# Masks and evictions moved, x transposed into token order, and router logits made by token

## The chip, the cores and the metric

The kernel runs on one core of a Trainium2 chip. The metric is the device time of one execution in microseconds (us); three runs were made and their median counts. Engines are named as in the profile: PE is TensorE, PEld its weight loads, DVE VectorE, ACT ScalarE, POOL GpSimd, SP the engine that issues most transfers.

## The reference

Attention with 4 batches, 8 heads, 576 positions and 64 columns per head; the first four heads see a window of 32 positions, the others every fourth position of a window of 128. Its output, 2304 tokens of 512 columns, goes through a mixture of 8 experts with one expert per token, and then through a pair of dense layers with a softplus between them.

```
mask_plain = (rel >= 0) & (rel < 32)
mask_dil = (rel >= 0) & (rel < 128) & (rel % 4 == 0)
x = softmax(where(mask, scale * q @ k.T, -1e9)) @ v     # (2304, 512)
logits = x @ w_gate;  e = argmax(logits)                # 8 experts
gate_w = softmax(logits)[e];  eom = sigmoid(x @ w_output_gate)
y = gate_w * eom[e] * (relu(x @ w1[e]) @ w2[e])
g = softplus(y @ w_in);  out = g @ w_out
```

## The kernel before

The attention is cut into 20 tiles: 4 batches b, five stretches w of 128 positions (the last has 64). A loop of 22 iterations runs them in a pipeline. Iteration i makes, in the order of the code: `scores` and `softmax` of tile i (products `s` on PE, maximum and subtraction on DVE), the transposes of the probabilities of tile i-1 (`pp`, evicted by ACT as `pt`), some units of the next batch's q and k (`pqk`), `exps` of tile i on ACT, `transpose_x` and `evict_x` of tile i-2 (`px` on PE, `xT` on ACT), then sums, values (`o` on PE) and `normalise` (`x` on DVE) of tile i-1, and the stores of x. A q/k unit transposes pieces of q or k on PE; `evict_qk` copies them to SBUF, k on ACT, q on DVE in batch 0 and in the dilated half, otherwise on ACT. The unit with y == 2 holds the last pieces of both q and k, and is evicted in four copies.

A tile of x has its rows in token order for heads 0 to 3, and in dilated order (row 32 r + m holds token 4 m + r) for heads 4 to 7. `px` is made of four products of 128 columns, c = 0 to 3; c = 2 and 3 belong to the dilated half.

The router handles the tiles in six groups, `GROUPS`: tiles 0 to 3, 4 to 7, 8 to 10, 11 to 13, 14 to 16 and 17 to 19, called groups 0 to 5 here and in the code. `logits_of` forms the logits `pl` with the 32 columns of `wg` standing still and the tile's x moving, in up to four column groups of PE side by side; c = 0, 1 and c = 2, 3 go to different columns of PSUM, since their tokens are in different orders. `logits` copies the first to `lt`, adds the second in token order, and has PE transpose the sum (`plt`). The generator `route` then makes, in small steps that the loop pumps between its own work, arg max, gate and rank of each token (`rmx`, `req`, `roh`, `rsel`, `prk`, `rgs`, `cumb`), and `rposi`. With rposi, POOL scatters one column per tile to `idx_dram` by an indirect DMA (L605). `W_LT` and `W_RANK` say how many steps a group's generator lets pass at two points.

After group 3's scatters POOL loads `idx` and gathers the first expert's rows (`xg`, L817). In the tail, group 5 is routed beside the products `xacc` that put rows of late tiles in place (L940, L992; `l` and `h` are the split operands of these); PE then goes on with the experts (`ph`, `py`) and from 395 us with the dense layers.

Of the kernel before, what the change touches and what calls it, by code (L numbers as in the profile page):

```python
# [11 lines left out]
F32 = mybir.dt.float32  # L12
# [4 lines left out]
ALU = mybir.AluOpType  # L17
# [4 lines left out]
P = 128  # L22
# [20 lines left out]
def attn_moe_softplus_kernel(ctx: ExitStack, tc: tile.TileContext, q, k, v, w_gate, w_ogate, w1, w2, w_in, w_out, out, dbg=None):  # L43
# [8 lines left out]
    NW = 5  # L52
# [63 lines left out]
            nc.sync.dma_start(wg[:, :, j * NE : (j + 1) * NE], w.rearrange("(c p) e -> p c e", p=P))  # L116

    def masks():
        nc.vector.tensor_copy(mask_0, mask_w)
        nc.vector.tensor_copy(mask_0[:32, 0], mask_w[:32, 1])  # L120

    def consts2():
        nc.gpsimd.memset(upper, 1.0)
# [172 lines left out]
    def transpose_qk(b, half, ti, y):  # L296

        own = b == 0 and (half, ti, y) in ((0, 0, 2), (1, 0, 2))  # L300
        ps = (ps_x0 if own else ps_t).tile([P, 512], F32, tag="x0" if own else "tp", name=f"pqk{b}{half}{ti}{y}")

        def to(t, y):
            dst = qT[b % 2][64 * y : 64 * y + 64, half] if t == 0 else kT[b % 2][64 * y : 64 * y + 64, half, :, y]
            return dst[:, :, :S].rearrange("q x (p j) -> q x p j", j=9)

        if y < 2:
            r = raw[b, half, ti].rearrange("p y e -> p (y e)")
            for j in range(4):
                c = 2 * D * (5 * y + j)  # L310
                nc.tensor.transpose(ps[:, P * j : P * j + P], r[:, c : c + 2 * D], identf)
            for o in range(2):
                src = ps[64 * o : 64 * o + 64].rearrange("q (j x p) -> q x p j", j=4, x=2)
                evict_qk(b, half, ti, to(ti, y)[:, :, :, y + o : y + o + 7 : 2], src)
        else:

            for t in range(2):
                r = raw[b, half, t].rearrange("p y e -> p (y e)")
                nc.tensor.transpose(ps[:, P * t : P * t + P], r[:, 8 * D : 10 * D], identf)
            for y in range(2):  # L320
                for t in range(2):
                    src = ps[64 * y : 64 * y + 64, P * t : P * t + P].rearrange("q (x p) -> q x p", x=2)
                    evict_qk(b, half, t, to(t, y)[:, :, :, 8 - 8 * y], src)

# [129 lines left out]
    def transpose_x(b, w):  # L454
        d = tl[b, w]
        x2 = d["x"].rearrange("q a h d -> q (a h d)")
        ps = ps_x0.tile([P, 512], F32, tag="x0", name=f"px{b}{w}")
        for c in range(4):
            nc.tensor.transpose(ps[:, P * c : P * c + P], x2[:, P * c : P * c + P], identf)
        d["xp"] = ps  # L460

    xT = {}
# [8 lines left out]

    def logits_of(*tiles_):

        for c in range(NC):
            for i in tiles_:
                g = next(g for g, (t0, t1) in enumerate(GROUPS) if t0 <= i < t1)
                j = i - GROUPS[g][0]
                if ("pl", g) not in xT:
                    xT["pl", g] = ps_t.tile([P, 2, P], F32, tag="tp", name=f"pl{g}")
                nc.tensor.matmul(  # L480
                    xT["pl", g][32 * j : 32 * j + 32, c // 2],
                    wg[:, c],
                    xT[g][:, j, P * c : P * c + P],
                    start=(c % 2 == 0),
                    stop=(c % 2 == 1),
                    skip_group_check=True,
                )

    def logits(g):
        n_ = GROUPS[g][1] - GROUPS[g][0]  # L490
        if g < G_FAST:
            logits_of(*range(*GROUPS[g]))
        pl = xT.pop(("pl", g))
        lt = xt_p.tile([P, P], F32, tag="lt", name=f"lt{g}")

        nc.vector.tensor_copy(lt[: 32 * n_], pl[: 32 * n_, 0])
        yield 0
        lt_ = lt[: 32 * n_].rearrange("q (m r) -> q m r", r=4)
        nc.vector.tensor_tensor(lt_, lt_, pl[: 32 * n_, 1].rearrange("q (r m) -> q m r", r=4), ALU.add)
        yield W_LT[g]  # L500
        pt = ps_t.tile([P, P], F32, tag="tp", name=f"plt{g}")
        nc.tensor.transpose(pt[:, : 32 * n_], lt[: 32 * n_], identf[: 32 * n_, : 32 * n_])
        xT[g] = pt.rearrange("q (j e) -> q j e", j=4)[:, :, : 2 * NE]
# [2 lines left out]

    K = {"rt": rt_p, "ixe": const}

    G_FAST, W_LT, W_RANK = 5, (6, 8, 1, 1, 1, 1), (8, 8, 3, 2, 2, 2)
    places, routed = {}, [0]  # L510

    scat = []
# [623 lines left out]
    for i in range(n + 2):  # L1136
        nqk = 0
        PUMP[0], PUMP[1] = (2, 1) if i < 12 else (4, 2) if i < n else (2, 2)
        if i == n - 5:
            rawx.close()  # L1140
            K["wr"] = rctx.enter_context(tc.tile_pool(name="wr", bufs=RB, side="right"))
        if i == n - 4:
            per0x.close()
            K["w1"] = rctx.enter_context(tc.tile_pool(name="w1", bufs=4, side="right"))
            pctx = ExitStack()
            for nm, bufs in (("xge", 4), ("sp0", 4), ("xl0", 5), ("sel", 4), ("rt2", 2)):
                K[nm] = pctx.enter_context(tc.tile_pool(name=nm, bufs=bufs, side="right"))
            K["slots"] = K["sel"].tile([P, CAPS[0]], F32, name="slots", bufs=1)
            nc.gpsimd.iota(K["slots"], [[1, CAPS[0]]], base=0, channel_multiplier=0, allow_small_or_imprecise_dtypes=True)
        if i < n:  # L1150
            b, w = tiles[i]
            if b + 1 < B:
                nqk = (QK_AT if b else QK_0)[w]
                if w == 0:
                    if b == 0:
                        fills(1)
                    todo += [(b + 1, *u_) for u_ in QK_UNITS]
            scores(b, w)
            softmax(b, w)
        if 1 <= i < n + 1:  # L1160
            transpose_p(*tiles[i - 1])
            evict_p(*tiles[i - 1])
        if i < n:
            pump()
        events(i, 0)
        some_qk(nqk - 1)
        if i < n:
            exps(*tiles[i])
        if 2 <= i:
            transpose_x(*tiles[i - 2])  # L1170
            evict_x(i - 2)
            pump()
        events(i, 1)
        if 1 <= i < n + 1:
            sums(*tiles[i - 1])
        events(i, 2)
        some_qk(min(nqk, 1))
        if 1 <= i < n + 1:
            values(*tiles[i - 1])
            normalise(*tiles[i - 1])  # L1180
        if i == 2:
            small_loads()
        if i < n and b + 1 < B:

            for half, heads in (((0, (0, 1)),), ((0, (2, 3)),), ((1, (0, 1)),), ((1, (2, 3)),), ())[w]:
                load_v(b + 1, half, heads)
            if w in (1, 3) and b + 2 < B:
                load_qk(b + 2, w // 2)
        events(i, 3)
        pump()  # L1190
        events(i, 4)
        pump()
        if i == n - 4:
            nc.vector.tensor_scalar(K["slots"], K["slots"], e0nt, None, ALU.add)
            K["rt"] = K["rt2"]
# [303 lines left out]
```

## Time and profile before

| what | value |
| --- | --- |
| time, median of 3 runs | 805.63 us (804.82 to 807.19) |
| the profiled execution | 805.44 us, span 803.7 us |
| PE busy | 767.2 us, 95% of the span |
| PEld busy | 690.7 us, 86% |
| DVE busy | 545.3 us, 68% |
| ACT busy | 478.8 us, 60% |
| POOL busy | 98.4 us, 12% |

The profile comes from one execution. Its instructions carry the line of the kernel and the names of the tiles; "idle before" is the time that an engine waited ahead of an instruction, and the arrow names what ended the wait. The chain of waits is followed back from the last instruction, at each step to what released it. Busy time is a union of overlapping instructions: PE's passes overlap, so the mean of one is longer than its share of the busy time. An F32 product can show as more than one pass in the records. A row of a stretch holds its bounds, its length, then busy time (instructions) of PE, PEld, DVE, ACT and POOL, the granted clock as a share of full, the DMA share and GB/s; asked for one line, only the engines that it uses.

### The profile page before, as it was taken

To read this page: it belongs to the slowest core of one execution; us is meant where nothing else is said; L and a number is where in the kernel's file an instruction comes from. 1 tells how busy PE (TensorE), PEld (TensorE's weight loads), DVE (VectorE), ACT (ScalarE), POOL (GpSimd) and SP (SyncE) were. 2 spreads that over 40 slices of the span, in tenths; PEclk is the share of its full clock that TensorE was granted. 3 is DMA by queue.
4 is the path that set the end of the run, shared out by engine and by line. 5 is a ranking of instruction groups with operands and counts; after the bars stand their busy time and mean duration, and the time that the engine had idled before them with its cause. 6 is when DMAs were issued, how large, how long until landed. Compare 5 with 4: busy or idle time off the path is not lost.

```text
span 803.7 us, 15090 instructions
## 1 busy us (share of the span) xinstructions
PE 767.2 (95%) x5542; PEld 690.7 (86%) x5543; DVE 545.3 (68%) x1098; ACT 478.8 (60%) x935; POOL 98.4 (12%) x124
## 2 busy tenths in 40 slices
PE   6998887899999999999999999999999999999996
PEld 5666655798999999999988999999999998999994
DVE  5766866773567877885688887766656656656552
ACT  4774623354656756666798877666546555555552
POOL 9502033321011011000000000020001001001001
PEclk7999999899999999999999999999999999999999
DMA  8979755366688999978624311310001001001001
GB/s 222 252 199 225 146 135 168 79 184 205 235 266 274 325 298 308 322 243 276 210 79 130 107 46 40 93 65 11 10 1 40 0 1 40 2 1 39 1 1 39
DMA packets 89039, 106.85 MB, mean 133 GB/s; under 512 B 29900, under 2 KB 64332, under 8 KB 88944
## 3 DMA queue, kind: packets, MB, share of 16 engines
q1 hardware_dynamic: 80448, 90.04, 37.7%
q0 software_dynamic: 3888, 10.12, 3.8%
q10 hardware_dynamic: 4608, 5.38, 1.9%
q8 instruction: 65, 1.06, 0.6%
q14 instruction: 30, 0.25, 0.1%
HBM read 85.03 MB, written 20.63 MB: 131 GB/s over the span
## 4 chain that ended last, share of the span: by engine, by line
PE 76%; issue 9%; ACT 5%; DVE 4%; DMA 4%; another core or an unknown queue 0%; POOL 0%; SPq 0%; ACTq 0%; POOLq 0%
PE pg L874 7%; PE pg L875 7%; PE pg L876 7%; PE q L1408 7%; PE q L1407 7%; PE q L1409 7%; PE s L364 3%; PE py L870 3%; PE py L871 3%; PE py L872 3%; PE ph L870 3%; PE ph L872 3%; PE ph L871 3%; PE o L419 2%; PE ph L874 1%
## 5 line engine op out<-in xcount | busy, mean ns | idle before, releaser
L874 PE MATMUL pg<-xhm,wh 128*128 128x384 f32 x384 | 129.5, 337 | 0.4 <-ACT l L1374 0.4
L875 PE MATMUL pg<-xlm,wh 128*128 128x384 f32 x384 | 129.6, 338 | 0.0
L876 PE MATMUL pg<-xhm,wl 128*128 128x384 f32 x384 | 129.4, 337 | 0.0
L707 DVE TENSOR_TENSOR wl<-wr,wh 128x1024 fp32r<-128x1024 f32 (+1 forms) x86 | 98.2, 1143 | 30.6 <-ACT wh L762 29.9
L1372 ACT ACTIVATE u<-pg 128x384 f32<-128x384 f32 x96 | 47.1, 491 | 116.7 <-PE pg L876 116.5
L1408 PE MATMUL q<-wl,gh 128*128 128x512 f32 x288 | 113.2, 393 | 0.0
L1407 PE MATMUL q<-wh,gh 128*128 128x512 f32 x288 | 113.0, 393 | 0.0
L1409 PE MATMUL q<-wh,gl 128*128 128x512 f32 x288 | 112.6, 391 | 0.0
L762 ACT CAST wh<-wr 128x1024 fp32r<-128x1024 f32 x74 | 77.2, 1049 | 15.0 <-DMA wr<-in_moe_w_dram 5.0
L1378 DVE TENSOR_SCALAR w<-u 128x384 f32<-128x384 f32 x68 | 24.6, 362 | 85.1 <-ACT u L1373 84.6
L874 PEld LDWEIGHTS pg<-xhm,wh 128*128 128x128 f32 x384 | 72.1, 188 | 4.9 <-ACT l L1374 1.0
L875 PEld LDWEIGHTS pg<-xlm,wh 128*128 128x128 f32 x384 | 72.0, 188 | 3.7
L876 PEld LDWEIGHTS pg<-xhm,wl 128*128 128x128 f32 x384 | 72.1, 188 | 0.0
L1416 POOL DMA_INDIRECT out_dram<-o,perm_sb x18 | 18.1, 1004 | 435.7 <-DVE o L255 303.0
L1380 DVE SCALAR_TENSOR_TENSOR u<-w,u 128x384 f32<-128x384 f32 x96 | 53.7, 559 | 21.6 <-ACT w L1376 19.3
L1409 PEld LDWEIGHTS q<-wh,gl 128*128 128x128 f32 x288 | 54.1, 188 | 12.3
L1407 PEld LDWEIGHTS q<-wh,gh 128*128 128x128 f32 x288 | 54.1, 188 | 8.6
L1408 PEld LDWEIGHTS q<-wl,gh 128*128 128x128 f32 x288 | 54.0, 188 | 8.2
L870 PE MATMUL ph<-xh,wh 128*128 128x392 f32 (+5 forms) x192 | 58.6, 305 | 1.6 <-ACT y L897 0.9
L1382 DVE TENSOR_TENSOR l<-l,u 128x384 f32<-128x384 f32 x96 | 53.5, 557 | 7.4
L870 PE MATMUL py<-hh,wh 128*128 128x312 f32 (+8 forms) x192 | 58.4, 304 | 0.0
L871 PE MATMUL py<-hl,wh 128*128 128x312 f32 (+4 forms) x192 | 57.3, 299 | 0.0
(204 smaller groups left out, 1722.9 us busy)
## 6 DMA issues: line engine op xcount, KB each, us to landing
wr<-in_moe_w_dram SPq DMA_DIRECT2D x64, 512.0 KB
praw<-in_moe_w_out_dram SPq DMA_DIRECT2D x12, 512.0 KB
raw<-in_q_dram SPq DMA_DIRECT2D x8, 576.0 KB
raw<-in_k_dram SPq DMA_DIRECT2D x8, 576.0 KB
x_dram<-x SPq DMA_DIRECT2D x36, 128.0 KB
x2r<-yT_dram SPq DMA_DIRECT2D x12, 384.0 KB
vP<-in_v_dram SPq DMA_DIRECT2D x16, 272.0 KB
praw<-in_moe_w_in_dram SPq DMA_DIRECT2D x8, 512.0 KB
```

The costliest lines, as they stand in the source:

```text
L707: e.tensor_tensor(lo, src, hi.bitcast(F32), ALU.subtract)
L762: (eng or nc.scalar.copy)(d[1], d[0])
L870: nc.tensor.matmul(ps if wide else ps[:, :cut], wh, xh if wide else xh[:, :cut], start=wide, stop=False, skip_group_check=True)
L871: nc.tensor.matmul(ps[:, :cut], wh, xl[:, :cut], start=False, stop=False, skip_group_check=True)
L874: nc.tensor.matmul(ps, wh, xh, start=(first and i == 0), stop=False)
L875: nc.tensor.matmul(ps, wh, xl, start=False, stop=False)
L876: nc.tensor.matmul(ps, wl, xh, start=False, stop=(last and i == k - 1))
L1380: nc.vector.scalar_tensor_tensor(u, w_, 1.0, u, ALU.subtract, ALU.subtract)
L1382: nc.vector.tensor_tensor(l, l, u, ALU.subtract)
L1407: nc.tensor.matmul(acc[b, t], gh[:, ts_], wh, start=(f == 0), stop=False)
L1408: nc.tensor.matmul(acc[b, t], gh[:, ts_], wl, start=False, stop=False)
L1409: nc.tensor.matmul(acc[b, t], gl[:, ts_], wh, start=False, stop=(f == NF - 1))
```

## The change

1. The two copies that make `mask_0` go from DVE to ACT.
2. The four evictions of a y == 2 unit are ordered q, q, k, k instead of q, k, q, k.
3. The products c = 2 and 3 of `px` are ordinary products against `turn`, the identity read in another column order, so that xT comes out in token order in all four parts.
4. `logits_of` sums all four c in one place of PSUM. The add in `logits` goes. For groups 3 to 5 (`G_ROWS` = 3) the tile's x stands still and 16 columns of `wg` move, so that the logits come out by token; for these groups the copy `lt` and the transpose `plt` go too.
5. `W_LT` and `W_RANK` of groups 1 and 2 change, and one unit of q/k in tile 4 comes earlier (`early`).

```diff
--- before.py
+++ after.py
@@ -116,8 +116,8 @@
             nc.sync.dma_start(wg[:, :, j * NE : (j + 1) * NE], w.rearrange("(c p) e -> p c e", p=P))
 
     def masks():
-        nc.vector.tensor_copy(mask_0, mask_w)
-        nc.vector.tensor_copy(mask_0[:32, 0], mask_w[:32, 1])
+        nc.scalar.copy(mask_0, mask_w)
+        nc.scalar.copy(mask_0[:32, 0], mask_w[:32, 1])
 
     def consts2():
         nc.gpsimd.memset(upper, 1.0)
@@ -317,8 +317,8 @@
             for t in range(2):
                 r = raw[b, half, t].rearrange("p y e -> p (y e)")
                 nc.tensor.transpose(ps[:, P * t : P * t + P], r[:, 8 * D : 10 * D], identf)
-            for y in range(2):
-                for t in range(2):
+            for t in range(2):
+                for y in range(2):
                     src = ps[64 * y : 64 * y + 64, P * t : P * t + P].rearrange("q (x p) -> q x p", x=2)
                     evict_qk(b, half, t, to(t, y)[:, :, :, 8 - 8 * y], src)
 
@@ -455,8 +455,12 @@
         d = tl[b, w]
         x2 = d["x"].rearrange("q a h d -> q (a h d)")
         ps = ps_x0.tile([P, 512], F32, tag="x0", name=f"px{b}{w}")
+        turn = identf.rearrange("q (r m) -> q m r", r=4)
         for c in range(4):
-            nc.tensor.transpose(ps[:, P * c : P * c + P], x2[:, P * c : P * c + P], identf)
+            if c < 2:
+                nc.tensor.transpose(ps[:, P * c : P * c + P], x2[:, P * c : P * c + P], identf)
+            else:
+                nc.tensor.matmul(ps[:, P * c : P * c + P], x2[:, P * c : P * c + P], turn, start=True, stop=True)
         d["xp"] = ps
 
     xT = {}
@@ -471,32 +475,31 @@
 
     def logits_of(*tiles_):
 
-        for c in range(NC):
-            for i in tiles_:
-                g = next(g for g, (t0, t1) in enumerate(GROUPS) if t0 <= i < t1)
-                j = i - GROUPS[g][0]
-                if ("pl", g) not in xT:
-                    xT["pl", g] = ps_t.tile([P, 2, P], F32, tag="tp", name=f"pl{g}")
-                nc.tensor.matmul(
-                    xT["pl", g][32 * j : 32 * j + 32, c // 2],
-                    wg[:, c],
-                    xT[g][:, j, P * c : P * c + P],
-                    start=(c % 2 == 0),
-                    stop=(c % 2 == 1),
-                    skip_group_check=True,
-                )
+        g = next(g for g, (t0, t1) in enumerate(GROUPS) if t0 <= tiles_[0] < t1)
+        cs = range(NC)
+        pairs = [(i, c) for i in tiles_ for c in cs] if g >= G_ROWS else [(i, c) for c in cs for i in tiles_]
+        for i, c in pairs:
+            j = i - GROUPS[g][0]
+            if ("pl", g) not in xT:
+                xT["pl", g] = ps_t.tile([P, P], F32, tag="tp", name=f"pl{g}")
+            pl, x_ = xT["pl", g], xT[g][:, j, P * c : P * c + P]
+            if g >= G_ROWS:
+                o, l, r = pl[:, 2 * NE * j : 2 * NE * j + 2 * NE], x_, wg[:, c, : 2 * NE]
+            else:
+                o, l, r = pl[32 * j : 32 * j + 32], wg[:, c], x_
+            nc.tensor.matmul(o, l, r, start=(c == 0), stop=(c == NC - 1), skip_group_check=True)
 
     def logits(g):
         n_ = GROUPS[g][1] - GROUPS[g][0]
         if g < G_FAST:
             logits_of(*range(*GROUPS[g]))
         pl = xT.pop(("pl", g))
+        if g >= G_ROWS:
+            xT[g] = pl[:, : 8 * NE].rearrange("q (j e) -> q j e", j=4)
+            return
         lt = xt_p.tile([P, P], F32, tag="lt", name=f"lt{g}")
 
-        nc.vector.tensor_copy(lt[: 32 * n_], pl[: 32 * n_, 0])
-        yield 0
-        lt_ = lt[: 32 * n_].rearrange("q (m r) -> q m r", r=4)
-        nc.vector.tensor_tensor(lt_, lt_, pl[: 32 * n_, 1].rearrange("q (r m) -> q m r", r=4), ALU.add)
+        nc.vector.tensor_copy(lt[: 32 * n_], pl[: 32 * n_])
         yield W_LT[g]
         pt = ps_t.tile([P, P], F32, tag="tp", name=f"plt{g}")
         nc.tensor.transpose(pt[:, : 32 * n_], lt[: 32 * n_], identf[: 32 * n_, : 32 * n_])
@@ -506,7 +509,8 @@
 
     K = {"rt": rt_p, "ixe": const}
 
-    G_FAST, W_LT, W_RANK = 5, (6, 8, 1, 1, 1, 1), (8, 8, 3, 2, 2, 2)
+    G_ROWS = 3
+    G_FAST, W_LT, W_RANK = 5, (6, 3, 2, 1, 1, 1), (8, 4, 3, 2, 2, 2)
     places, routed = {}, [0]
 
     scat = []
@@ -1163,7 +1167,8 @@
         if i < n:
             pump()
         events(i, 0)
-        some_qk(nqk - 1)
+        early = nqk if i == NW - 1 else max(nqk - 1, 0)
+        some_qk(early)
         if i < n:
             exps(*tiles[i])
         if 2 <= i:
@@ -1174,7 +1179,7 @@
         if 1 <= i < n + 1:
             sums(*tiles[i - 1])
         events(i, 2)
-        some_qk(min(nqk, 1))
+        some_qk(min(nqk - early, 1))
         if 1 <= i < n + 1:
             values(*tiles[i - 1])
             normalise(*tiles[i - 1])
```

What moves on PE, at the logits of group 3 (tiles 11 to 13): the rows from `s` of a tile to `o` of the tile before it. Before:

```order
L364 MATMUL s_1808<-kT_120,qT_118 32x128 x16
L392 MATMUL pp_1830<-identf,p_1704 128x128 x4
L480 MATMUL pl_1837<-xT_1513,wg 32x128 x12
L459 MATMUL px_1854<-identf,x_1783 128x128 x4
L502 MATMUL plt_1865<-identf,lt_1850 128x96
L419 MATMUL o_1868<-vP_122,pt_1835 32x2x64 x8
L419 MATMUL o_1868<-vD_124,pt_1835 32x2x64 x8
```

With the change:

```order
L364 MATMUL s_1805<-kT_120,qT_118 32x128 x16
L392 MATMUL pp_1827<-identf,p_1701 128x128 x4
L490 MATMUL pl_1834<-wg,xT_1532 128x16 x12
L461 MATMUL px_1848<-identf,x_1780 128x128 x2
L463 MATMUL px_1848<-identf,x_1780 128x128 x2
L419 MATMUL o_1882<-vP_122,pt_1832 32x2x64 x8
L419 MATMUL o_1882<-vD_124,pt_1832 32x2x64 x8
```

The transpose `plt` between `px` and `o` is gone, `pl` has x standing still, and `px` is made of two pairs.

What moves on DVE, around the end of iteration 12. x_1447 before and x_1445 with the change are `normalise` of tile 11; the rows of `rgs` to `cumb` belong to group 1's router. Before:

```order
L442 TENSOR_TENSOR x_1447<-o_1430,rc_1413 128x512
L378 TENSOR_REDUCE mx_1473<-s_1455 128x8
L379 TENSOR_TENSOR p_1474<-mx_1473,s_1455 128x512
L496 COPY lt_1497<-pl_1484 96x128
L499 TENSOR_TENSOR lt_1497<-lt_1497,pl_1484 96x128
L427 TENSOR_REDUCE sm_1515<-p_1364 128x8
L428 TENSOR_SCALAR sm_1515<-sm_1515 128x8
L431 RECIPROCAL rc_1516<-sm_1515 128x2x2x2
L292 TENSOR_SCALAR qT_118<-pqk_1522 64x2x64 x2
L442 TENSOR_TENSOR x_1546<-o_1529,rc_1516 128x512
L571 TENSOR_REDUCE rgs_1398<-rsel_1403 128x4
L574 TENSOR_REDUCE rcb_1406<-roh_1405 128x8
```

With the change:

```order
L442 TENSOR_TENSOR x_1445<-o_1428,rc_1417 128x512
L575 TENSOR_REDUCE rgs_1316<-rsel_1321 128x4
L578 TENSOR_REDUCE rcb_1324<-roh_1323 128x8
L580 TENSOR_REDUCE rden_1315<-rex_1320 128x4
L582 TENSOR_TENSOR cumb<-cumb,rcb_1324 128x8
L585 TENSOR_TENSOR rpm_1322<-prk_1447,roh_1323 128x32
L587 TENSOR_SCALAR rgs_1316<-rgs_1316 128x4
L590 TENSOR_REDUCE rm_1314<-rpm_1322 128x4
L592 SCALAR_TENSOR_TENSOR rs_1317<-rden_1315,rgs_1316 128x4
L594 RECIPROCAL pair<-rs_1317 128x4
L606 CAST rposi_1325<-rm_1314 128x4
L378 TENSOR_REDUCE mx_1493<-s_1475 128x8
```

The steps `rgs` to `cumb` of group 1 stood behind x of tile 12 (x_1546); they now stand behind x of tile 11. `rposi`, for which POOL's four scatters of group 1 wait, follows there, ahead of the softmax of tile 13. The rows of SP and POOL stand in the same order as before.

## Rows read from the trace of the kernel before

**Rows 1.** Before and after 160 us: length, busy by engine, clock, DMA.
```profile
0.00:160.00 160.00, 134.48 (x1907) 99.92 (x1908) 109.71 (x309) 81.52 (x151) 56.66 (x85) 0.93 0.71 179
160.00:803.70 643.70, 632.68 (x3637) 590.77 (x3635) 435.55 (x790) 397.26 (x786) 41.73 (x39) 1.00 0.37 121
```

**Rows 2.** Chain of waits to the first `s`: start, length, what.
```profile
2.49 9.70 DMA raw<-in_k_dram
...
16.98 0.40 DVE qT L292
```

**Rows 3.** Chain of waits around tiles 4 and 5.
```profile
42.33 0.40 DVE qT L292
...
45.36 0.44 PE px L459 x4
```

**Rows 4.** Chain of waits around 97 us.
```profile
96.37 0.40 DVE qT L292
...
99.43 0.59 ACT pt L401
```

**Rows 5.** Chain of waits from 101 to 125 us.
```profile
101.47 0.69 PE s L364 x15
...
106.11 1.14 PE s L364 x11
...
113.54 1.04 PE pl L480 x24
...
115.57 1.01 PE o L419 x32
...
116.90 1.50 PE s L364 x32
...
124.31 0.59 ACT pt L401
```

**Rows 6.** Timeline of GpSimd: start, length, instruction [idle before, releaser].
```profile
100.22 0.90 POOL L605 DMA_INDIRECT idx_dram<-pair,rposi  x1 [24.43 <-DVE rposi L602]
...
107.30 0.96 POOL L605 DMA_INDIRECT idx_dram<-pair,rposi  x1 [2.39 <-DVE rposi L602]
...
135.98 1.00 POOL L817 DMA_INDIRECT xg<-x_dram,idx  x1 [2.80 <-DMA idx<-idx_dram]
```

**Rows 7.** Chain of waits from 138 to 157 us.
```profile
138.29 3.68 another core or an unknown queue
...
146.44 1.91 PE xacc L940 x8
...
156.06 0.76 DVE l L973
```

**Rows 8.** Three stretches at half clock, columns as in Rows 1.
```profile
76.50:79.80 3.30, 3.21 (x47) 2.10 (x47) 1.27 (x3) 0.00 (x0) 0.00 (x0) 0.50 0.85 267
107.20:110.50 3.30, 3.30 (x38) 3.00 (x41) 2.55 (x7) 1.59 (x3) 2.59 (x3) 0.50 0.28 80
141.40:148.10 6.70, 4.68 (x20) 3.67 (x21) 3.65 (x13) 1.82 (x3) 2.90 (x3) 0.50 0.38 110
```

**Rows 9.** Groups of TensorE up to 160 us: passes, busy, mean, idle.
```profile
L459 PE MATMUL px<-identf,x 128*128 128x128 f32 x80 | 13.2, 291 | 4.6 <-DVE x L442 4.6
L480 PE MATMUL pl<-xT,wg 128*32 128x128 f32 x160 | 11.2, 296 | 3.1 <-issue 1.5 <-ACT xT L470 1.4
```

**Rows 10.** Passes of `s` of one tile: contiguous half, then dilated.
```profile
L364 PE MATMUL s<-kT,qT 128*32 128x128 f32 x16 | 0.6, 279 | 0.0
...
L364 PE MATMUL s<-kT,qT 128*32 128x128 f32 x16 | 1.1, 405 | 0.0
```

**Rows 11.** TensorE and its weight loads in eight passes of L940.
```profile
151.94:152.84 0.90, 0.90 (x9) 0.90 (x8) 1.00 0.00 0
```

**Rows 12.** Timeline of VectorE, second mask copy.
```profile
6.76 2.02 DVE L120 COPY mask<-mask_w 32x64 bf16<-32x64 bf16 x1
```

**Rows 13.** Timeline of TensorE, `s` of tile 5.
```profile
43.18 1.15 PE L364 MATMUL s<-kT,qT 128*32 128x128 f32 x16 [1.54 <-ACT kT L290]
```

## The prediction

> **What bounds the kernel now.** I read the table of stretches first [rows 1]. From 160 us on TensorE is busy 632.68 of 643.70 us at full clock: none of the edits touches that work, so the change is decided before 160 us. There TensorE is also the fullest engine, 134.48 us against 109.71 of VectorE and 81.52 of ScalarE, but it is not busy throughout: 25.5 us of the first 160 are idle. So TensorE work added is not hidden by rule; it is hidden only where the chain of waits leaves TensorE. That chain was read second, stretch by stretch: in most iterations it runs through TensorE alone, and it leaves it at four kinds of places. (a) Around the last q/k unit of a batch, where ScalarE and VectorE hand each other single evictions of about 0.4 us [rows 2, 3, 4]. (b) Before `o`, where ScalarE's eviction of pt has to come first [rows 5]. (c) After indirect DMAs on GpSimd: the four of group 1 start at 100.22, one about every 1.26 us, and group 2's first at 107.30 [rows 6]. The products `s` of one tile, 1.50 us at 116.90 [rows 5], run from 101.47 to 107.25 there, 5.78 us, with pieces of "issue" between them. (d) At 138.29, where VectorE waits 3.68 us for a releaser that the profile can't name, while the gathers run [rows 7]. The clock comes third: half of full (1.2 GHz of 2.4) in 76.5 to 79.8, 107.2 to 110.5 and 141.4 to 148.1, each time after TensorE had been halting or idle [rows 8].
>
> The profiled execution took 805.44 us: the span of 803.70 and 1.74 outside it. The median of the runs is 805.63, so the sum below is made from 805.44.
>
> **The turning products** (dearer). Of four products that transpose a tile of x, two become ordinary F32 products whose moving operand is the identity read with a step of 128 bytes. The records hold 80 passes for 80 transposes but 160 passes for the 80 logits products [rows 9], so an ordinary F32 product is two passes. What a pass with a step costs stands in one place only: the dilated half of `s` reads k with a step of four elements. Its passes have a mean of 405 ns, those of the contiguous half 279 [rows 10]. Passes go in waves of four, so the 126 ns are added to a wave. A contiguous pass of 128 columns is 0.109 us (px, four of them, is 0.44 [rows 3]), so one with a step is 0.235. Then px is 2 x 0.109 + 4 x 0.23 = 1.14 us instead of 0.44: +0.70 a tile, 14 us of TensorE work over 20 tiles. Bounds: if the step costs nothing it is +0.22; if 32 elements cost twice what 4 do, +1.6. I take the row, since it is the same engine and type. The Trainium skill speaks against this edit ("SBUF — State Buffer", Specifications): full bandwidth takes at least two hits in each 16-byte line, so F32 read more than a few elements apart pays on each. By that page, read as a pass of twice 0.109, px would be 1.09, an estimate 0.4 us below mine over the path; the row decides.
>
> Where does it show? px stands on the chain nine times, as at 45.36 [rows 3]. One, at 66.92, comes behind a wait on x that the new order of evictions shortens, so it is left out, and the one at 130.71 is counted with group 4: 7 x 0.70 = **+4.9**. In two iterations px lies under the wait for pt, as at 124.31 [rows 5], 0.68 with the gaps around it: only 1.14 - 0.68 comes out, 2 x 0.46 = **+0.9**. In the others TensorE waits for other work before and after.
>
> **Logits with x standing still** (groups 3 to 5). A product now loads 128 columns of x and moves 16 of wg. Such a load-bound pass is seen in xacc L940 with 40 moving columns: 8 passes in 0.90 us, 0.112 each [rows 11]. The 24 passes of a group of three tiles then take 2.69; now they take about 1.0, as at 113.54 [rows 5], because three column groups run at once. The copy, the add and plt fall away. Group 3: from pl at 113.54 to `o` at 115.57 is 2.03 now [rows 5]; then it is 2.69 + 1.14 = 3.83: **+1.8**. Group 4: pl +1.69 by the same sum, px +0.70, one plt pass of 0.1 less: **+2.3**. Group 5's tiles are done one by one already, where pl of a tile is load-bound too: nothing. Bounds: if the load of x hid behind the pass before, 24 x 0.03 would make both groups about 2 cheaper each; the 0.90 shows that it doesn't.
>
> Added in all: 4.9 + 0.9 + 1.8 + 2.3 = 9.9 us.
>
> **Masks and evictions.** The second mask copy on VectorE ends at 8.8 (6.76 + 2.02), and the chain to the first `s` starts from the raw k that lands at 12.19 [rows 2]: moving the copies is worth nothing [rows 12]. ScalarE has both behind its table load, ahead of its first eviction; they would cost up to their 2 us each only if ScalarE were not through with them and its first evictions by 12.33. With q,q,k,k one eviction of VectorE, 0.40 at 16.98, and the gaps beside it no longer stand between two of ScalarE: **-0.45** [rows 2]. In tile 4 both units come early, and the last kT stands no longer behind p and xT of ScalarE: `s` starts at 43.18 now after TensorE has idled 1.54 [rows 13]. With the kT straight behind its unit, near 41.5, TensorE's own px and o become the limit: **-1.1** (0 to -1.5). At the start of batch 2 the order in VectorE's row before x is shorter too; in iterations 12 and 13 fourteen steps of the router stand on the chain behind qT at 96.37 and x, ahead of pt at 99.43 [rows 4]: **-0.8** (0 to -1.6).
>
> **Scatters earlier.** The router of group 1 runs an iteration earlier, as VectorE's rows above show: its scatters come behind x of tile 11, not close to those of group 2. The work that they hold up is the same, but TensorE may not halt for so long that the clock falls. Of 4.3 us of halting (5.78 - 1.50) and 1.6 us at the lower clock (half of 3.30 busy) [rows 6, 8] I take **-2** (0 to -5.9), a third, since the four scatters still stand one behind another.
>
> **The wait at 138.29.** Its end hangs on the gathers, those on group 3's scatters, which come about 1.5 us earlier in their iteration. TensorE, late by 5 to 6 us, reaches `o` of the last tile later, and the 3.68 us are used up by its own work: **-2.9** (0 to -3.4) [rows 7]. What is late next is x of the last tile, px, pl.
>
> **The tail.** px, pl and xacc behind the wait run at half clock, xacc 1.91 against 0.90 for eight such passes at full clock [rows 7, 11]. If TensorE no longer idles ahead of them, pl and xacc are about 0.95 shorter each; half of it, **-1** (0 to -1.95). The copy, the add and plt between pl and lg are gone, so lg comes ahead of xacc instead of behind it, over 2 us earlier; but TensorE works on xacc meanwhile and can win only its later waits for `l`, the last of them ending with the piece at 156.06: **-0.85** by their sum, with 0 if `l` waits for h [rows 7].
>
> Taken off: 0.45 + 1.1 + 0.8 + 2 + 2.9 + 1 + 0.85 = 9.1. Sum: 805.44 + 9.9 - 9.1 = **806.2 us**.
>
> **The rivals.**
> Slower: the indirect DMAs stay serial with TensorE. The gathers start only after rposi of group 3 and the load of idx behind it; if these are late by as much as TensorE is, the wait at 138.29 moves with it and covers nothing, and the scatters of group 1 halt TensorE for as long in another iteration. Then -2, -2.9 and -1 fall away: 812.1. For it: VectorE, which makes rposi, itself waits for TensorE's `o`; against it: group 3's scatters move ahead within the iteration. It decides once the gathers start more than 4 us after their 135.98 of now [rows 6].
> Faster by the step: a single product may read with a step at no cost, the 405 ns coming from four products reading at once. Then px is +0.22: 1.5 + 0 + 1.3 + 1.8 = 4.6 instead of 9.9, 800.9 us. For it: no single stepped pass is in the trace. Against: half the data rate fits each of the four as well as all.
> Faster by the clock: with fuller TensorE rows none of the falls after 20 us happens. Those stretches hold 3.21, 3.30 and 4.68 us of busy time [rows 8], so 5.6 us at most, of which some 1.7 stands in the sum: 802.3. For it: the falls came after halts; against: the halts of the scatters stay. The Trainium skill ("TensorE: Matmul & The Clock Gate", Part 4: PE-mode transpose) says that a transposing pass doesn't count for the clock as an ordinary one does, by which the new products would help to hold it up; the trace does not bear it out so far, as the mean clock of the first 160 us is 0.93 [rows 1] with transposes throughout.
> Nothing of it: added and removed work both lie in TensorE's idle 25.5 us, and the time stays at 805.4. It cannot be told from the forecast.
>
> **How the numbers follow.** A difference under 0.3% (2.4 us) can hardly be told from no change. The forecast, with its own range of 803.2 to 808.0 and the case of nothing in it: 0.36. The slower rival 0.32; faster by the step 0.17; by the clock or by scatters wholly apart 0.15. Bounds: all uncertain gains nil 812.1, all full 805.44 + 9.9 - 14.5 = 800.8. Leaving a tenth out at each end, 801 to 811.5.
>
> **What would show it.** px near 1.1 us per tile on the chain (0.7 means the step is free); pl of groups 3 and 4 near 2.7; no idle TensorE before `s` of tile 5; group 1's scatters an iteration ahead of group 2's and full clock near 108; TensorE at o of the last tile near 144 with no 3.7 us wait ahead. It is wrong if a single stepped pass is as quick as a contiguous one, or if the gathers' start moves by as much as TensorE's lateness.

## The result and the profile after

The changed kernel takes 811.14 us (median of 7 runs, 810.32 to 817.14); the kernel before took 805.56 in the 7 runs beside it. The ratio is 1.0092 with an interval of 1.0073 to 1.0111: slower by 5.9 to 8.9 us. The forecast was 806.2, no difference that can be told, with a range of its own from 803.2 to 808.0. The profiled execution has a span of 808.8 us, 5.1 more than before.

The whole difference lies ahead of the first expert. Its first product `ph` starts at 160.00 before and at 164.67 after, +4.67 of the 5.1. The last tile's `s`, beginning with its mask product, starts at 125.96 before and 127.81 after, +1.85; the other 2.8 us are lost between there and `ph`.

The stretches of the changed kernel, with the columns of [rows 1]:

```profile
0.00:160.00 160.00, 142.25 (x1919) 109.13 (x1921) 102.97 (x293) 82.33 (x150) 55.17 (x77) 0.93 0.74 176
160.00:808.80 648.80, 637.07 (x3662) 595.30 (x3660) 437.72 (x795) 398.13 (x787) 44.31 (x48) 1.00 0.38 121
```

TensorE is busy 7.8 us longer in the first 160 us, VectorE 6.7 us less: the change moves work from the engine with room to the fullest one.

The timeline of TensorE at group 3's logits in the changed kernel (start, length, instruction), for the place of [rows 5] at 113.54:

```profile
112.04 2.75 PE L490 MATMUL pl<-wg,xT 128*128 128x16 f32 x24
114.64 0.42 PE L461 MATMUL px<-identf,x 128*128 128x128 f32 x2
114.89 1.04 PE L463 MATMUL px<-identf,x 128*128 128x128 f32 x4
115.86 0.64 PE L419 MATMUL o<-vP,pt 128*32 128x128 f32 x16
```

From pl to `o` are 3.82 us, where the prediction had 3.83 and before took 2.03. Both new prices are there as they were worked out: 24 passes whose weight loads take 2.76 us, 0.112 apart, and px at 1.22 from its start to `o`, gaps included.

What was not expected stands further on. The same timeline in the tail, and then three stretches of it:

```profile
126.80 0.65 PE L419 MATMUL o<-vP,pt 128*32 128x128 f32 x16 [1.50 <-ACT pt L401]
...
130.95 2.90 PE L490 MATMUL pl<-wg,xT 128*128 128x16 f32 x24
133.70 0.41 PE L461 MATMUL px<-identf,x 128*128 128x128 f32 x2
133.95 1.04 PE L463 MATMUL px<-identf,x 128*128 128x128 f32 x4
135.67 1.89 PE L490 MATMUL pl<-wg,xT 128*128 128x16 f32 x8 [0.68 <-ACT xT L474]
...
141.18 0.69 PE L461 MATMUL px<-identf,x 128*128 128x128 f32 x2 [0.58 <-DVE x L442]
...
143.41 1.89 PE L490 MATMUL pl<-wg,xT 128*128 128x16 f32 x8 [0.68 <-ACT xT L474]
145.23 1.08 PE L419 MATMUL o<-vP,pt 128*32 128x128 f32 x16
...
148.19 0.48 PE L461 MATMUL px<-identf,x 128*128 128x128 f32 x2 [0.20 <-DVE x L442]
```

```profile
126.80:130.80 4.00, 4.00 (x69) 3.00 (x70) 2.96 (x6) 3.00 (x4) 0.00 (x0) 0.63 0.43 94
134.70:148.30 13.60, 11.47 (x100) 8.68 (x99) 4.75 (x27) 1.97 (x5) 6.75 (x7) 0.50 0.40 124
152.00:155.00 3.00, 3.00 (x16) 2.53 (x15) 2.12 (x17) 1.07 (x4) 0.00 (x0) 0.50 0.11 37
```

The work there runs at half clock: 11.47 us of busy time from 134.7 to 148.3, where [rows 8] had 4.68 from 141.4 to 148.1. A single tile's pl takes 1.89, where the first one of group 5 before took 0.95:

```profile
131.97 0.95 PE L480 MATMUL pl<-xT,wg 128*32 128x128 f32 x7 [0.24 <-ACT xT L470]
```

TensorE's wait for x ahead of the last px, 3.53 us before, is gone, as foreseen: only 0.58 and 0.20 are left. But VectorE's long wait, which runs while GpSimd gathers, has not gone; it has moved to another tile. These are the last two `x` in VectorE's timeline, before and then with the change:

```profile
133.99 0.69 DVE L442 TENSOR_TENSOR x<-o,rc 128x512 f32<-128x512 f32 x1 [1.58 <-PE o L419]
142.00 0.69 DVE L442 TENSOR_TENSOR x<-o,rc 128x512 f32<-128x512 f32 x1 [3.71 <-remote]
```

```profile
140.43 0.69 DVE L442 TENSOR_TENSOR x<-o,rc 128x512 f32<-128x512 f32 x1 [4.89 <-PE prk L574]
147.44 0.69 DVE L442 TENSOR_TENSOR x<-o,rc 128x512 f32<-128x512 f32 x1 [3.80 <-PE o L419]
```

Before, the last of the four gathers ends on GpSimd at 140.72, and only the last tile's x comes behind it. With the change it ends at 139.52, and the x of the tile before the last comes behind it too, so that px, pl and `o` of that iteration and the last x follow, 7.0 us more. The stretch from the last `s` to the last px, in the columns of [rows 1], before and then with the change:

```profile
125.96:142.74 16.78, 10.64 (x165) 7.60 (x162) 8.54 (x33) 5.39 (x10) 4.99 (x6) 0.96 0.55 162
```

```profile
127.81:148.19 20.38, 18.25 (x169) 14.51 (x165) 8.81 (x38) 5.83 (x11) 7.57 (x8) 0.58 0.39 116
```

Two rows of GpSimd's timeline in the changed kernel, for [rows 6]:

```profile
93.49 0.91 POOL L609 DMA_INDIRECT idx_dram<-pair,rposi  x1 [16.92 <-DVE rposi L606]
...
134.76 1.02 POOL L821 DMA_INDIRECT xg<-x_dram,idx  x1 [1.84 <-DMA idx<-idx_dram]
```

Group 1's scatters start 6.7 us earlier than before, and the gathers 1.2 us earlier in spite of a later TensorE.

### The profile page after: what moved, and what is told of

The parts are those of the page before. It is cut to its first block, busy times and chain, and to the rows that moved or that the text cites. A ratio compares the mean times of both kernels' runs of the same rounds, so it can differ in the third digit from the quotient of the medians.

```text
span 808.8 us, 15158 instructions
## 1 busy us (share of the span) xinstructions
PE 779.3 (96%) x5579; PEld 704.4 (87%) x5580; DVE 540.7 (67%) x1087; ACT 480.5 (59%) x937; POOL 99.5 (12%) x124
## 3 DMA queue, kind: packets, MB, share of 16 engines
q8 instruction: 65, 1.06, 0.6%
## 4 chain that ended last, share of the span: by engine, by line
PE 61%; issue 8%; DVE 2%; ACT 2%; DMA 1%; POOL 0%; ACTq 0%; POOLq 0%
PE pg L878 7%; PE pg L879 7%; PE pg L880 7%; PE q L1413 7%; PE q L1412 7%; PE q L1414 7%; PE ph L874 3%; PE ph L876 3%; PE ph L875 3%; PE py L874 3%; PE py L875 3%; PE py L876 3%; DMA yT_dram<-y 1%; PE px L839 1%; ACT wh L766 1%
```

## The experiments

Ratios are to runs of the kernel before, made beside those of each kernel. These took about 805 us in the first two sets (experiments 1 to 7 and 10), on two chips, and 795 to 798 in the last two (8, 9, 11 and 12), on a third, so only ratios are compared across sets. Even these have to be read with care: VectorE's long wait for an unnamed releaser beside the gathers is in the traces of before, of the change and of the first two sets, and in none of the four from the third chip. A point is a hundredth of the time of before, so 0.1 points are 0.8 us.

Four theories of the loss were set against each other. A: the new work on TensorE is paid on the path, the stepped products above all (and, A', the load-bound ones). B: the loss is made in the tail, by waits, and the early scatters only change what they hold up. C: products with 16 moving columns lower the clock of the work behind them. D: the clock falls because TensorE waits, for pt behind group 3's scatters.

**1. Evictions and masks alone** (the kernel before with three edits):

```diff
-        nc.vector.tensor_copy(mask_0, mask_w)
+        nc.scalar.copy(mask_0, mask_w)
...
-            for y in range(2):
-                for t in range(2):
+            for t in range(2):
+                for y in range(2):
...
-        some_qk(nqk - 1)
+        early = nqk if i == NW - 1 else max(nqk - 1, 0)
+        some_qk(early)
...
-        some_qk(min(nqk, 1))
+        some_qk(min(nqk - early, 1))
```

> The kernel before with the masks on ScalarE, the evictions q,q,k,k and both units early in tile 4, nothing else. Theory A (hand-overs on the path are gained): 1.5 to 2.4 us faster than before, 803 to 804. Theory B (what is gained at the start and in tile 4 is lost again in the waits for the scatters and gathers): within 1 us of before, 804.5 to 806.5.

Measured: 803.22 us, ratio 0.9977 (0.9962 to 0.9992). Theory A fits, though the interval, 0.6 to 3.1 us, reaches into Theory B's. In its timeline of TensorE `s` of tile 5 has no idle time ahead of it, where [rows 13] had 1.54:

```profile
39.20 0.62 PE L419 MATMUL o<-vD,pt 128*32 128x128 f32 x16
39.75 0.39 PE L351 MATMUL s<-mask,identb 128*128 128x512 bf16 x1
40.07 1.74 PE L364 MATMUL s<-kT,qT 128*32 128x128 f32 x32
```

**2. Scatters as before.** The step counts of before in the changed kernel:

```diff
-    G_FAST, W_LT, W_RANK = 5, (6, 3, 2, 1, 1, 1), (8, 4, 3, 2, 2, 2)
+    G_FAST, W_LT, W_RANK = 5, (6, 8, 1, 1, 1, 1), (8, 8, 3, 2, 2, 2)
```

> The changed kernel with the step counts W_LT and W_RANK of before, so that group 1 is routed and scattered an iteration later again. Theory A (the earlier scatters gain what the prediction took, 2 us): slower, 812 to 814. Theory B (the scatters only change which work they hold up): within 1.5 us of 811, with the halting of TensorE again near the scatters, and g3's scatters at another place of iteration 18.

Measured: 812.92 us, ratio 1.0094 (1.0070 to 1.0117), against 1.0092 with the change's counts. Theory B: the 2 us are not to be seen in this kernel, within about 0.3 points.

**3. Group 3's scatters later:**

```diff
-    G_FAST, W_LT, W_RANK = 5, (6, 3, 2, 1, 1, 1), (8, 4, 3, 2, 2, 2)
+    G_FAST, W_LT, W_RANK = 5, (6, 3, 2, 1, 1, 1), (8, 4, 3, 5, 2, 2)
```

> The changed kernel with W_RANK of group 3 at 5 instead of 2, so that its three scatters start behind x of tile 16, as before, and not ahead of the sums. Theory D (the scatters at 121.4 to 124.9 hold back px and pt, TensorE idles 1.5 us at 126.8 and the clock falls): no wait for pt there, full clock around 128, and 806 to 809. Theory C: the wait may go, but the clock still falls behind pl of group 4, and the time stays at 809 to 812.

Measured: 813.00 us, ratio 1.0107 (1.0077 to 1.0136). The wait of 1.50 for pt is down to 0.21, and nothing is gained. TensorE's timeline shows that the same scatters now hold up `o`:

```profile
126.32 0.64 PE L419 MATMUL o<-vP,pt 128*32 128x128 f32 x16 [0.21 <-ACT pt L401]
126.78 0.61 PE L419 MATMUL o<-vD,pt 128*32 128x128 f32 x13
127.82 0.27 PE L419 MATMUL o<-vD,pt 128*32 128x128 f32 x1 [0.44 <-issue]
128.54 0.39 PE L419 MATMUL o<-vD,pt 128*32 128x128 f32 x2 [0.45 <-issue]
```

Theory D falls as the main cause: with the wait gone, the clock is at half from 136 to 148 all the same.

**4. The turned identity without a step.** A tile of its own, written once at the start; the products stay ordinary ones:

```diff
+    turnf = const.tile([P, P], F32, name="turnf")
...
+        nc.vector.tensor_copy(turnf.rearrange("q (m r) -> q m r", r=4), identf.rearrange("q (r m) -> q m r", r=4))
...
-        turn = identf.rearrange("q (r m) -> q m r", r=4)
+        turn = turnf
```

> The changed kernel with the turned identity kept as a tile of its own, so that the products against it read it without a step; still ordinary F32 products, two passes each. Theory A (the step is paid on the path): px falls from 1.13 to about 0.66 us a tile, and of 20 x 0.46 some 7 to 10 show, so the time falls by 3 to 5 us, to 806 to 808. Theory B (the loss is made in the tail, by a wait for pt at 126.8 and by half clock from 127 to 155): px falls as much, but the time by less than 2 us as long as TensorE idles there.

Measured: 809.17 us, ratio 1.0040 (1.0019 to 1.0060): 0.52 points off 1.0092, Theory A. Its timeline of TensorE, same place as above:

```profile
112.20 0.41 PE L463 MATMUL px<-identf,x 128*128 128x128 f32 x2
112.45 0.61 PE L465 MATMUL px<-turnf,x 128*128 128x128 f32 x4
112.99 0.64 PE L421 MATMUL o<-vP,pt 128*32 128x128 f32 x16
```

From px to `o` are 0.79 us instead of 1.22: the four passes without a step are 0.43 shorter. So a single product reading with a step pays too, and the rival by which it would read freely is out. The Trainium skill ("SBUF — State Buffer", Specifications) asks for at least two hits in each 16-byte line for full bandwidth. The trace agrees in kind: up to the start of `o`, the four passes take 0.97 with the step and 0.54 without.

**5. No logits by token** (`G_ROWS = 6`, so that wg stands still in all groups):

> The changed kernel with the logits of groups 3 to 5 made as in groups 0 to 2 (wg stands still, copy lt and transpose plt). Theory A' (load-bound passes are paid on the path): pl of groups 3 and 4 falls from 2.7 to 1.0 us, less what lt and plt cost (about 0.7 each): 1.5 to 3 us faster, 808 to 809.5. Theory B: within 1 us of the changed kernel, 810 to 812, or slower by lt and plt in the tail.

Measured: 804.28 us, ratio 0.9990 (0.9971 to 1.0008). The logits by token cost 1.02 points in the changed kernel, with an uncertainty of about 0.3, over twice what either theory gave them. TensorE's timeline shows pl at 1.07 and a wait for x again, of 3.51, as before the change; VectorE's long wait stands at the last tile's x again, at 142.15:

```profile
129.14 1.07 PE L490 MATMUL pl<-xT,wg 128*32 128x128 f32 x24
...
142.89 0.44 PE L461 MATMUL px<-identf,x 128*128 128x128 f32 x2 [3.51 <-DVE x L442]
```

**6. By token in group 5 alone** (`G_ROWS = 5`):

> The changed kernel with logits by token for group 5 alone; groups 3 and 4 have wg standing still. pl of groups 3 and 4 is 1.0 us. Theory C: half clock only behind the single tiles' products from 132 us on; first ph near 162. Theory D: group 3's scatters come behind px again, no wait for pt at 126 to 128, clock as in the kernel with no logits by token, first ph near 160.

One run: 804.65 us, first `ph` at 158.92. There is no wait for pt, as Theory D had it; half clock comes behind the single tiles' products, from 136 to 148, as Theory C had it. It doesn't decide between the two. A single run within the range of before (803.25 to 807.99 beside it) suggests that groups 3 and 4 carry most of the cost, and that these 12 us at half clock need not cost anything: the long wait is at the last tile's x here.

**7. The same products with more columns.** x stands still, but the 32 columns of wg are read four times over:

```diff
...
-                o, l, r = pl[:, 2 * NE * j : 2 * NE * j + 2 * NE], x_, wg[:, c, : 2 * NE]
+                o, l, r = pl[:, P * j : P * j + P].rearrange("q (a e) -> q a e", a=4), x_, wg[:, c].unsqueeze(1).to_broadcast([P, 4, 32])
...
```

> The changed kernel, but each product of groups 3 to 5 moves 128 columns (the 32 of wg, read four times over) instead of 16; only the first 16 columns that come out are used. The load of x, 0.112 us a pass, stays the limit, so a group of three still takes 2.7 us. Theory C (after the products with 16 moving columns the clock falls, and that is most of the 6.8 us that the logits by token cost): full clock between 130 and 145 us and 805 to 808. Theory D (the clock falls because TensorE waits there, 1.5 us for pt and 0.7 us for each xT): the same half clock as in the changed kernel, and 810 to 812.

Measured: 809.04 us, ratio 1.0049 (1.0028 to 1.0071). The stretch from 130 to 142 us in the changed kernel, and the same in this one with rows of its timelines:

```profile
130.00:142.00 12.00, 10.75 (x91) 9.36 (x88) 5.14 (x22) 3.06 (x7) 4.66 (x5) 0.64 0.38 119
```

```profile
130.00:142.00 12.00, 7.73 (x83) 6.30 (x82) 5.46 (x29) 2.95 (x7) 4.63 (x5) 1.00 0.40 118
```

```profile
125.00 1.08 PE L419 MATMUL o<-vP,pt 128*32 128x128 f32 x16 [1.54 <-ACT pt L401]
...
129.59 2.84 PE L490 MATMUL pl<-wg,xT 128*128 128x128 f32 x24
...
140.14 0.44 PE L461 MATMUL px<-identf,x 128*128 128x128 f32 x2 [3.05 <-DVE x L442]
```

```profile
139.39 0.69 DVE L442 TENSOR_TENSOR x<-o,rc 128x512 f32<-128x512 f32 x1 [5.21 <-remote]
146.47 0.69 DVE L442 TENSOR_TENSOR x<-o,rc 128x512 f32<-128x512 f32 x1 [3.87 <-PE o L419]
```

pl takes as long as with 16 columns, and the clock stays at full in this stretch. Theory C is right on the clock here, and Theory D wrong: the wait of 1.5 us for pt is in both kernels. Theory D fits a shorter fall, right behind that wait: half clock from 127.5 to 131.5 in the changed kernel and from 125.0 to 128.5 in this one, where the clock falls again at 142.0 and 148.5, behind waits for x of 3.05 and 0.91. Full clock doesn't bring the time of before back. TensorE is through with `o` of the tile before the last at 136.38 instead of 139.42, but its x comes only at 139.39, once the gathers are through (138.36), and from the last `s` to the last px it takes 20.34 us, as with half clock (20.38). Timed, the columns are worth 0.43 points, with an uncertainty of about 0.3, and 809.0 lies outside what C expected. The other 0.59 points stay with the products' length and their place.

**8. and 9. The pair again, with px back at 0.44 us.** The turned identity of its own is used in a transposing product (`nc.tensor.transpose(..., turnf)`), logits by token once with 16 and once with 128 columns:

> The changed kernel with a turned identity of its own and transposing products for c = 2 and 3 (px 0.44 us, as before); logits of groups 3 to 5 by token with 16 moving columns, as in the change. What remains of the change's loss is then the logits' alone. Theory C (16 moving columns: 2 x 1.7 us of load-bound passes, and the clock falls behind each pl): 806 to 808, half clock behind pl of group 4. Theory A (the turned products made nearly all of the loss): 801 to 803.

> As the one before, with 128 moving columns (wg four times over) instead of 16 in the logits by token. Theory C: 2 to 4 us faster than with 16 columns, with full clock behind pl of group 4; 803 to 805. If the fall of the clock hangs on the waits and not on the columns: the same time and clock as with 16.

Measured: 0.9977 (0.9941 to 1.0013) with 16 columns, 0.9935 (0.9911 to 0.9960) with 128; 0.42 points again, but the intervals overlap, so this pair alone doesn't settle it. On the scale of 805.4 the first is 803.6, between the two theories; the logits by token cost only 0.39 points over experiment 10 here, with an uncertainty of 0.4, and with 128 columns nothing that shows. Three stretches with 16 columns, the first with group 3's pl and the last behind group 4's, then two stretches with 128 and the same work:

```profile
103.00:107.90 4.90, 4.90 (x68) 4.30 (x64) 3.85 (x15) 1.75 (x3) 1.23 (x2) 0.99 0.59 31
107.90:110.60 2.70, 2.70 (x46) 1.76 (x42) 1.90 (x9) 0.46 (x3) 0.00 (x0) 0.50 0.73 235
...
124.50:128.80 4.30, 4.14 (x50) 3.36 (x49) 1.88 (x9) 0.91 (x3) 2.13 (x3) 0.60 0.62 188
```

```profile
103.00:110.00 7.00, 7.00 (x108) 5.86 (x106) 5.43 (x20) 2.33 (x6) 0.30 (x1) 1.00 0.70 149
117.00:129.00 12.00, 10.29 (x139) 8.20 (x131) 7.51 (x34) 4.24 (x9) 4.36 (x5) 1.00 0.53 150
```

With 16 columns the clock falls behind either group's pl, the first time with TensorE busy in all of the 4.90 us ahead; with 128 it doesn't. On this chip x does not wait for the gathers: in experiment 9 they run from 124.54 to 129.27, and the last tile's x starts among them, as soon as its `o` is there:

```profile
128.35 0.69 DVE L444 TENSOR_TENSOR x<-o,rc 128x512 f32<-128x512 f32 x1 [1.00 <-PE o L421]
```

**10. Transposing products, no logits by token:**

> No logits by token, and the turned identity a tile of its own, used in a transposing product (one pass without a step) for c = 2 and 3: px is back at 0.44 us, xT is in token order, and the add in logits is gone. By the prices found so far (turned products about 4 us, evictions 1.5 us gained) 800 to 802; if the turned products' price was their place beside the scatters and not their length, 803 to 805.

Measured: 799.85 us, ratio 0.9938 (0.9919 to 0.9958). It is faster than both kernels, and 0.52 points under experiment 5, which differs in px alone. Its timeline of px, two passes and two:

```profile
109.30 0.44 PE L463 MATMUL px<-identf,x 128*128 128x128 f32 x2
109.58 0.38 PE L465 MATMUL px<-turnf,x 128*128 128x128 f32 x2
```

**11. Ordinary products without a step, no logits by token:**

> No logits by token; the products for c = 2 and 3 are ordinary ones, two passes, but against a turned identity of its own, without a step: px 0.66 us. It stands between the same kernel with the step (1.13 us, ratio to before 0.999) and that with transposing products (0.44 us, 0.9938). If the step is what the turned products cost, in proportion to TensorE's time two thirds of the 0.52 points come back: 0.995 to 0.996. If the second pass or the clock weighs as much: 0.997 or above.

Measured: 0.9943 (0.9920 to 0.9967). Level with 0.9938, which was measured on another chip: it is the step that the turned products cost. A price of the second pass can't be told, with an uncertainty of 0.3 points, in which the 2 us that the sum gave it would lie.

**12. Transposing products, 128 columns, group 5 alone by token:**

> The transposing products with a turned identity of its own, logits by token for group 5 alone, with 128 moving columns: in the tail lg comes right behind pl, without lt and plt. Theory C: no fall of the clock but those that group 5's waits make, and 798.5 to 800.5, level with or 1 us under the kernel without logits by token. If products with x standing still lower the clock whatever moves: 801 to 804.

Measured: 0.9951 (0.9923 to 0.9980), level with 0.9938, 0.9935 and 0.9943. The copy and the transpose of the last group's logits are worth nothing that shows.

## Why the prediction was wrong

Split at the last `s` and at the last px, the sum of the prediction and the profiles compare as follows, in us. The terms are placed where they act: of the seven 0.70 of px, six lie ahead of the last `s` and one, for the last tile, behind the last px's start.

| stretch | forecast | came |
| --- | --- | --- |
| up to the last `s` | +2.55 | +1.85 |
| from there to the last px | -0.6 | +3.60 |
| from there to `ph` | -1.15 | -0.78 |

The miss lies in the middle, where the sum has only group 4's logits with their px, +2.3, and the wait at 138.29, -2.9.

**The step that failed first: the wait at 138.29, -2.9.** The sum kept this wait at the last tile's x and let TensorE's lateness use it up. TensorE was late, and the gathers came 1.2 us earlier. So the wait fell on the x of the tile before the last, 4.89 us at 140.43, and px, pl, `o` and the last x came behind it. In the change's profile the `o` of that tile ends at 139.42 and the gathers at 139.52, so TensorE's own lateness and the gathers hold it about alike; in experiment 7, at full clock, only the gathers do. The ten traces from outside the third chip agree. In the five kernels without logits by token in groups 3 and 4 (before, experiments 1, 5, 6 and 10) the x that starts just behind the gathers is the last one; in the five with them (the change, experiments 2, 3, 4 and 7) it is the one before, and the last x follows 7.0 to 7.1 us later. What the profile doesn't name is why x waits for the gathers, and no run moved the gathers alone, so the size of this cost is read from traces and not timed. The gathers did not move back with TensorE, so the slower rival is wrong in that, though it gives 812.1, near the measured time. Its other half, that the scatters hold TensorE up for as long elsewhere, is borne out by experiment 2.

**The second: the clock in the tail.** The sum counted the logits of groups 4 and 5 at full clock (+2.3 and nothing), and took -1 because "If TensorE no longer idles ahead of them, pl and xacc are about 0.95 shorter each". The last pl and its eight xacc passes did become shorter, 1.06 and 1.52 us instead of 1.91 and 1.98. But the work ahead of them, which had run at full clock, now ran at half, although TensorE idled less: from the last `s` to the last px the mean clock is 0.58 instead of 0.96. The change's own products were not asked what they do to the clock.

**Logits with x standing still: right in length, wrong in cost.** 2.69 us were forecast for a group and 2.75 came. In the changed kernel they cost 1.02 points, some 8 us. The 16 columns are worth 0.4 points of it, some 3.4 us, in both pairs, but in the profiles of the pairs the stretch from the last `s` to the first `ph` is as long with full clock as with half (36.7 and 36.9 us in the first pair, 30.1 in both of the second). The rest is not the length alone, since in experiment 9 products as long cost nothing that shows, on the chip without the long wait. That fits the tile that slips behind the gathers. Where in the span the timed 0.4 points are made stays open.

**Evictions: right.** -0.45, -1.1 and part of -0.8 were forecast; -1.9 us came, by 0.23 points.

**The turning products: right in kind, a little large.** The pass with a step was taken from four products that read at once, and held for one. The step was forecast at 5.3 us (the 9.9 of the sum less the 4.6 of the rival by which it is free) and cost 0.47 to 0.52 points, 3.8 to 4.2 us, each with an uncertainty of about 0.3 points. What the second pass cost is not shown.

**Scatters earlier, -2: not found in the changed kernel.** 1.0094 and 1.0092 with either order. The scatters hold up whatever TensorE does beside them, s, px, pt or o: experiments 2 and 3 only change which. Experiment 10 is 0.39 points under experiment 1; whether earlier scatters or the missing add make that was not tested.

Two bounds of the prediction don't come out of its terms: with all gains that have a range at nothing the sum is 814.9 and not 812.1, and with all at full 799.7 and not 800.8. The rivals by the clock and by a free step were both wrong, and so was the one that nothing comes of it. The Trainium skill ("TensorE: Matmul & The Clock Gate", Part 4: PE-mode transpose) says that transposing passes don't count for the clock as ordinary ones do. No such difference shows here: the mean clock of the runs is 0.988 to 0.993 with transposing turned products (experiment 10), and 0.988 to 0.996 with ordinary ones (experiments 5 and 11).

## What to carry to other kernels

An operand that is read with a step on the fullest engine is paid at each use; here, writing the permuted identity once as a tile of its own took back all of the price that shows. Exchanging the standing and the moving operand is judged by its passes and not by its columns, and by the granted clock of the work behind them. A gain that rests on covering a wait should be counted with what the cover itself costs: if either changes, both terms do. And where the wait comes at a time of its own, as beside the gathers here, ask which tile will stand in it once an engine is late.

## What was not expected of the hardware

The weight loads of 24 passes take 2.76 us with 16 moving columns and with 128, 0.112 apart. Behind the former the granted clock fell to 0.50, in experiment 8 with no idle time in the 4.90 us ahead; behind the latter it stayed at 1.00 (experiments 7 and 9). It did not fall each time: with 16 columns it fell behind group 4's pl in five of five profiles, behind group 3's in two of five (experiments 3 and 8).

And while GpSimd's indirect transfers run, what waits for a product goes on late. In the changed kernel group 3's three scatters are on GpSimd from 121.41 to 124.92. TensorE's `s` ends at 123.41 and its pp at 124.00, by the profile, and TensorE itself works on; but VectorE's maximum of s starts at 126.05 and ScalarE's copy of pp at 126.16, where the copy of the tile before started at 119.58, 0.75 behind the start of its pp. Here is the px that they are put down to, which took until 125.30, and then the two that waited:

```profile
124.18 1.12 PE L463 MATMUL px<-identf,x 128*128 128x128 f32 x4
```

```profile
126.05 0.69 DVE L378 TENSOR_REDUCE mx<-s 128x8 f32<-128x512 f32 x1 [3.11 <-PE px L463]
```

```profile
126.16 0.59 ACT L401 COPY pt<-pp 128x512 f32<-128x512 f32 x1 [4.59 <-PE px L463]
```

With these scatters moved away (experiment 3) TensorE's wait for pt falls from 1.50 to 0.21. What holds the signal up is not shown.
